# One ring of PSUM tiles for all stages, and K in bundles of four: a convolution and channel mix fused on one core

## The chip, the cores, the metric

One core of one Trainium2 chip runs the whole kernel. The metric is device time in microseconds (us); lower is better. Each time below is the median of the runs named beside it. TensorE does the matmuls, VectorE (DVE) and ScalarE (ACT) read their results out of PSUM, GpSimd (POOL) and SyncE (SP) mostly issue transfers.

## The reference, cut to what matters

```python
# x: (8, 4160, 192) f32; 8 heads of 24 channels, 7 taps each
w = softmax(weight, axis=-1)
y[b, s, h, :] = sum(w[h, k] * x_pad[b, s + k, h, :] for k in range(7))   # causal
xk = mu_k * y + (1 - mu_k) * y_prev       # y_prev: y one token earlier
xr = mu_r * y + (1 - mu_r) * y_prev
k = relu(xk @ w_k)                        # 192 -> 1024
v = (k * k) @ w_v                         # 1024 -> 192
out = sigmoid(xr @ w_r) * v
```

## The kernel before

The eight sequences go through in four pairs. A pair is cut into steps of 512 tokens (the first pair begins and ends with a step of 256) and a tail of 64 tokens, because 4160 is 8 x 512 + 64. For each step TensorE computes, interleaved with its neighbours in time:

- the convolution `ps_c` (a matmul with a banded matrix), which ScalarE copies to `y`; `y` goes to DRAM and comes back transposed as `yT` (the first groups of the first pair are transposed on TensorE instead);
- K (`ps_k`) in slots of 2 x 512 columns, whose relu is on ScalarE and whose square is on VectorE;
- R (`ps_r`) with its sigmoid on ScalarE;
- V (`ps_v`) from the squares; VectorE multiplies it by the sigmoid into `o_sb`, which is stored.

From `yT` VectorE makes the difference `d` and the mixes `xk` and `xr`. The contraction of K is 192 = 128 + 64: a "hi" matmul of full height, and a "lo" pair of half height that runs side by side on the two halves of the array (row-tiled; in the trace they have 64 rows each, and the two of a pair start 3 or 4 ns apart, where two of full height and 512 columns start 216 apart). Parts that the change touches, cuts marked with `# ...`:

```python
psK = ctx.enter_context(tc.tile_pool(name="psK", bufs=3, space=bass.MemoryType.PSUM))  # K, R, conv: 3 x 2 banks
psV = ctx.enter_context(tc.tile_pool(name="psV", bufs=2, space=bass.MemoryType.PSUM))  # V, transposes: 2 x 1 bank

def k_section(ns):                 # a bundle: three slots (or two)
    # ...
    for n in ns[:-1]:
        k_mm(n, True, True)        # hi
    for n in ns[:-1]:
        k_mm(n, False, False)      # lo, row-tiled
    k_mm(ns[-1], False, True)      # lo, row-tiled
    k_mm(ns[-1], True, False)      # hi

def r_mm(m0):                      # R of four tiles, or of a tail, in a tile of psK
    ps = psK.tile([P, 2, BANK], FP32, tag="k", name="ps_r")
    # ...
def v_mm(m):                       # V of one tile of 128 tokens; a pair shares a bank of psV
    # ...
    if t % 2 == 0:
        v_ps[q] = psV.tile([P, 2, D], FP32, tag="v", name="ps_v")
    # ...

# the schedule, by slots n
at(dve, xs[-1] + 1, y_write, g)
at(dve, xs[-1] + (3 if g == 4 else 9), y_read, g)   # the transposed read, 8 slots after the write
# ...
at(xt, 2 if s == 0 else vs - 3, r, m)               # R and its sigmoid, 3 slots ahead of V
at(pe, vs, v_mm, m)                                 # V, one tile at a time
```

Of the kernel before, what the change touches and what calls it, by code (L numbers as in the profile page):

```python
# [14 lines left out]
def kernel(  # L15
# [29 lines left out]
    WARM = 20  # L45
# [5 lines left out]
    eight = ctx.enter_context(tc.tile_pool(name="eight", bufs=8))  # L51
    psK = ctx.enter_context(tc.tile_pool(name="psK", bufs=3, space=bass.MemoryType.PSUM))
    psV = ctx.enter_context(tc.tile_pool(name="psV", bufs=2, space=bass.MemoryType.PSUM))
# [17 lines left out]

    groups = []
    for p in range(NPAIR):
        blk0 = 0
        for nb, s, on_pe in (
            ((3, 0, True), (4, 1, True), (4, 2, True), (5, 3, True), (10, 4, False), (9, 6, False))
            if p == 0
            else ((10, 0, False), (10, 2, False), (10, 4, False), (5, 7, False))
        ):
            groups.append((p, blk0, nb, steps[first_step[p] + s][3], on_pe))  # L80
            blk0 += nb
# [52 lines left out]
    w_all = const.tile([P, H, K, 8], FP32)  # L134
# [61 lines left out]
    def make_toe():  # L196
# [4 lines left out]
            in0=w_nrm.unsqueeze(3).to_broadcast([P, H, K, 8]),  # L201
            in1=bass.AP(tensor=m.tensor, offset=m.offset, ap=[m.ap[0], [0, H], [1, K], [1, 8]]),
            op=ALU.mult,
        )
        with nc.allow_low_precision(reason="a sum of one number and zeros"):
            nc.vector.tensor_reduce(
                out=w_per,
                in_=w_all.rearrange("p h k r -> p h r k"),
                axis=mybir.AxisListType.X,
                op=ALU.add,  # L210
            )
# [18 lines left out]
    def conv_mm(g, c):  # L230
        nb = groups[g][2]
        if c == 0:
            ys[g] = two.tile([P, GB, 2 * D], BF16, tag="y", name="y")
        ps2 = psK.tile([P, 2, BANK], FP32, tag="k", name="ps_c")
        for k, hs in enumerate(chunks(g)[c : c + 2]):
# [3 lines left out]
            for i, h in enumerate(hs):  # L239
# [6 lines left out]
                )  # L246

# [40 lines left out]
    tr_ps = {}  # L288

    def tr_mm(g, j):  # L290
# [3 lines left out]
        ps = psV.tile([P, 3, 2, BLK], BF16, tag="v", name="ps_t")  # L294
        tr_ps[g, j] = ps
        for i in range(min(2, nb - 2 * j)):
            for c in range(3):
                nc.tensor.transpose(
                    out=ps[:, c, i, :],
                    in_=ys[g][:BLK, 2 * j + i, c * P : (c + 1) * P],  # L300
                    identity=ident[:BLK, :BLK],
                )

    def tr_out(g, j, copy):
        p, blk0, nb, _, _ = groups[g]
        ps = tr_ps.pop((g, j))
        n = min(2, nb - 2 * j)
        c0 = YC + (blk0 + 2 * j) * BLK
        copy(  # L309
            out=yTs[p][:, :, c0 : c0 + n * BLK].rearrange("p c (n t) -> p c n t", n=n),  # L310
            in_=ps[:, :, :n, :],
        )
# [16 lines left out]
    def mix(s, i, part):  # L329
# [4 lines left out]
        if part == 0 and L > TAIL:  # L334
            if i == 0:
                xks[s] = two.tile([P, 3, STEP], BF16, tag="xk", name="xk")
            else:
                xrs[s] = three.tile([P, 3, STEP], BF16, tag="xr", name="xr")
# [29 lines left out]
    def k_mm(n, hi, start):  # L368
# [5 lines left out]
        if start:  # L374
            k_ps[n] = psK.tile([P, 2, BANK], FP32, tag="k", name="ps_k")
# [15 lines left out]
    def k_section(ns):  # L391
# [4 lines left out]
        for n in ns[:-1]:  # L396
            k_mm(n, True, True)
        for n in ns[:-1]:
            k_mm(n, False, False)
        k_mm(ns[-1], False, True)  # L400
        k_mm(ns[-1], True, False)

    def k_mm_tail(n, p):
        ps = psK.tile([P, NF, 2 * TAIL], FP32, tag="k", name="ps_k")
# [38 lines left out]
    tiles = []  # L443
    for s, (p, t0, L, n0, ns) in enumerate(steps):
        for t in range(max(1, 2 * L // P)):
            at_ = n0 + ns + 1
            tiles.append((s, t, max(at_, tiles[-1][2] + 1) if tiles else at_))

    r_ps, r_sbs, v_ps = {}, {}, {}


    def r_mm(m0):
        s, _, _ = tiles[m0]
        p, _, L, _, _ = steps[s]
        ps = psK.tile([P, 2, BANK], FP32, tag="k", name="ps_r")
        r_ps[m0] = ps
        for k in range(4 if L > TAIL else 1):
            t = tiles[m0 + k][1]
            o = ps[:, k // 2, k % 2 * D : (k % 2 + 1) * D]
            if L > TAIL:  # L460
                xr = xrs[s]
                st, c = divmod(t * P, L)
                hi, lo, wlo = xr[:, st, c : c + P], xr[:, 2, c : c + P], wr[:, 2 + st, :]
            else:
                hi, lo, wlo = tails[p % 2][:, 1, 1, :], tails[p % 2][:, 1, 0, :], wr[:, 1, :]
            nc.tensor.matmul(out=o, lhsT=hi, rhs=wr[:, 0, :], start=True, stop=False)  # L466
            nc.tensor.matmul(out=o, lhsT=lo, rhs=wlo, start=False, stop=True)  # L467

    def r_sig(m0):
        ps = r_ps.pop(m0)  # L470
        if steps[tiles[m0][0]][2] > TAIL:
            r_sb = three.tile([P, 2, 2 * D], BF16, tag="r_sb", name="r_sb")
            nc.scalar.activation(out=r_sb, in_=ps[:, :, 0 : 2 * D], func=AF.Sigmoid)  # L473
            for k in range(2):
                r_sbs[m0 + 2 * k] = r_sb[:, k, :].rearrange("p (t d) -> p t d", t=2)
        else:
            r_sb = two.tile([P, D], BF16, tag="r_tail", name="r_tail")
            nc.scalar.activation(out=r_sb, in_=ps[:, 0, 0:D], func=AF.Sigmoid)
            r_sbs[m0] = r_sb.unsqueeze(1)

    def v_mm(m):
        s, t, _ = tiles[m]
        q = m - t % 2
        if t % 2 == 0:
            v_ps[q] = psV.tile([P, 2, D], FP32, tag="v", name="ps_v")
        o = v_ps[q][:, t % 2, :]
        k2 = k2s[s]
        for f in range(NF):
            nc.tensor.matmul(  # L489
                out=o,  # L490
                lhsT=k2[:, f, t * P : (t + 1) * P],
# [5 lines left out]
    def v_out(m):  # L497
        s, t, _ = tiles[m]
        p, t0, L, _, _ = steps[s]
        n = 2 if L > TAIL else 1  # L500
        o_sb = eight.tile([P, 2, D], FP32, tag="o_sb", name="o_sb")
        nc.vector.tensor_tensor(  # L502
            out=o_sb[:, :n, :], in0=v_ps.pop(m)[:, :n, :], in1=r_sbs.pop(m)[:, :n, :], op=ALU.mult
        )
        if L > TAIL:
            st, c = divmod(t * P, L)
            nc.sync.dma_start(
                out=out[2 * p + st, t0 + c : t0 + c + 2 * P, :].rearrange("(m p) d -> p m d", p=P),
                in_=o_sb,
            )  # L510
        else:
            for i in range(2):
                nc.sync.dma_start(
                    out=out[2 * p + i, t0:S, :], in_=o_sb[i * TAIL : (i + 1) * TAIL, 0, :]
                )


    early, xt, pe, dve = ({} for _ in range(4))

    def at(table, n, fn, *a):  # L520
        table.setdefault(n, []).append((fn, a))
# [6 lines left out]
    def r(m0):  # L528
        r_mm(m0)
        r_sig(m0)  # L530

    def tr(g, j):
        tr_mm(g, j)
        tr_out(g, j, nc.vector.tensor_copy)

    for g, (p, blk0, nb, n0, on_pe) in enumerate(groups):
        nx = -(-len(chunks(g)) // 2)
        ntr = (nb + 1) // 2
        if g == 0:
            continue  # L540
        if g == 1:
            xs, trs = [], [0] * ntr
        elif on_pe:
            xs = [[0, 1], [4, 6]][g - 2]
            trs = [[2, 3], [7, 8, 9]][g - 2]
        else:
            xs = {28: [7, 9, 11, 13], 44: [14, 16, 18, 20]}[n0] if p == 0 else range(n0 - 38, n0 - 38 + 4 * nx, 4)
            trs = []
            at(dve, xs[-1] + 1, y_write, g)

            at(dve, xs[-1] + (3 if g == 4 else 9), y_read, g)
        if g > 3:

            n = {4: 4, 5: 5, 6: 9, 7: 32, 8: 42, 9: 53}.get(g) or steps[first_step[p]][3] + (-63, -47, -31, -14)[(g - 6) % 4]
            at(early, n, x_tile, g, nc.vector)
            at(early, n, load_x, g)
        for i, n in enumerate(xs):
            at(xt, n, conv, g, 2 * i)
        for j, n in enumerate(trs):
            at(pe, n, tr, g, j)  # L560
    for s, (p, t0, L, n0, ns) in enumerate(steps):
        if s == 0:
            when = (None, None, None, 1, 1)
        elif s == 1:
            when = (0, 0, 1, 4, 5)
        elif s == 2:
            when = (5, 6, 7, 9, 10)
        elif n0 == 28:
            when = (22, 24, 25, 27, 28)
        else:  # L570
            when = (n0 - 8, n0 - 6, n0 - 5, n0 - 3, n0 - 2)
        if when[0] is not None:
            at(dve, when[0], diff, s)
        for n, (i, part) in zip(when[1:], ((0, 0), (0, 1), (1, 0), (1, 1))):
            if n is not None:
                at(dve, n, mix, s, i, part)
    for m, (s, t, vs) in enumerate(tiles):
        if t % 4 == 0:
            at(xt, 2 if s == 0 else vs - 3, r, m)
        if t % 2 == 1 or steps[s][2] == TAIL:  # L580
            at(dve, vs + 1, v_out, m - t % 2)
        at(pe, vs, v_mm, m)

    def run(table, n):
        for fn, a in table.get(n, ()):
            fn(*a)

    def warm(n):
        ps = psV.tile([P, BANK], FP32, tag="v", name="warm")
        for _ in range(n):  # L590
            nc.tensor.matmul(out=ps, lhsT=ones_t, rhs=zeros, start=True, stop=True)  # L591

    def prologue():
# [38 lines left out]
        dve_, act_ = nc.vector.tensor_copy, nc.scalar.copy  # L632
# [85 lines left out]
```

## Time and profile before

| | before |
|---|---|
| time, first three runs | 454.83 us (454.81 to 454.86) |
| span in the trace | 453.3 us |
| busy: TensorE, VectorE, ScalarE | 97%, 85%, 78% |
| granted TensorE clock | 1.00 |

Timeline columns: start, duration, engine, line, operation, output<-inputs, shapes, count, and in brackets the idle time before it and what ended it.

### The profile page before, as it was taken

The numbers are of one execution on the slowest core, as the hardware profiler recorded it, in microseconds if no ns is written. First come the engines' busy times: TensorE is split into PE (matmuls) and PEld (weight loads), VectorE is DVE, ScalarE is ACT, GpSimd is POOL, SyncE is SP. The second block draws the span as 40 slices with busy tenths as digits, with TensorE's granted clock in tenths as the row PEclk, the third lists the DMA queues.
The fourth block names the chain that finished last, engine by engine and source line by source line (L and its number), as shares of the span: only waits on it lengthen the run. The fifth ranks groups of instructions, "written<-read, shape, count | busy, mean of one in ns | idle before, by whom it ended". The sixth has DMA issues, their size and how long they took to land.

```text
span 453.3 us, 10019 instructions
## 1 busy us (share of the span) xinstructions
PE 441.0 (97%) x3942; PEld 301.8 (67%) x3942; DVE 385.1 (85%) x762; ACT 355.8 (78%) x464; POOL 48.6 (11%) x70
## 2 busy tenths in 40 slices
PE   7889999999999999999999999999999999999996
PEld 3555666767876676676676776776676776767676
DVE  4799489897989879888998888897998997988963
ACT  3779987888887787888887887888887877767771
POOL 8550001102030100102020010100200000000000
PEclk9999999999999999999999999999999999999999
DMA  8999869799598694957769793957655573421223
GB/s 90 146 170 137 149 190 168 151 192 186 135 179 177 165 180 108 156 137 145 170 140 161 182 184 108 147 135 189 111 135 136 142 152 94 109 71 53 72 71 97
DMA packets 134177, 63.66 MB, mean 140 GB/s; under 512 B 85714, under 2 KB 133874, under 8 KB 134130
## 3 DMA queue, kind: packets, MB, share of 16 engines
q1 hardware_dynamic: 95906, 48.33, 43.0%
q0 software_dynamic: 38224, 14.68, 28.5%
q8 instruction: 31, 0.51, 0.5%
q14 instruction: 16, 0.13, 0.1%
HBM read 29.39 MB, written 36.99 MB: 146 GB/s over the span
## 4 chain that ended last, share of the span: by engine, by line
PE 87%; DVE 8%; DMA 3%; ACT 1%; issue 1%; DVEq 0%
PE ps_k L383 36%; PE ps_v L489 35%; PE ps_r L466 4%; PE ps_r L467 4%; PE ps_c L240 4%; DVE k L440 3%; PE warm L591 2%; DMA yT<-y_dram 2%; DMA y_dram<-y 1%; DVE d L322 1%; DVE yT L309 1%; PE ps_k L409 1%; DVE o_sb L502 1%; DVE xk L364 1%; DVE xr L361 1%
## 5 line engine op out<-in xcount | busy, mean ns | idle before, releaser
L421 ACT ACTIVATE k_sb<-ps_k 128x1024 bf16<-128x1024 f32 x260 | 248.3, 1025 | 56.6 <-PE ps_k L383 52.6
L383 PE MATMUL ps_k<-xk,wk 128*128 128x512 bf16 (+3 forms) x1056 | 199.3, 374 | 0.5 <-ACT k_sb L421 0.4
L489 PE MATMUL ps_v<-wv,k 128*128 128x192 bf16 x2048 | 195.1, 246 | 2.3 <-DVE k L440 1.0
L489 PEld LDWEIGHTS <-k 128*128 128x128 bf16 x2048 | 172.8, 98 | 26.6 <-DVE k L440 1.6
L440 DVE TENSOR_TENSOR k<-k_sb 128x1024 bf16<-128x1024 bf16 x256 | 172.3, 684 | 4.6 <-ACT k_sb L421 4.3
L383 PEld LDWEIGHTS <-wk 128*128 128x128 bf16 (+1 forms) x1056 | 63.0, 96 | 104.7 <-issue 72.8
L502 DVE TENSOR_TENSOR o_sb<-ps_v,r_sb 128x384 f32<-128x384 f32 x128 | 70.9, 554 | 43.2 <-PE ps_v L489 41.0
L473 ACT ACTIVATE r_sb<-ps_r 128x768 bf16<-128x768 f32 x64 | 52.8, 825 | 16.9 <-PE ps_r L467 14.9
L466 PE MATMUL ps_r<-wr,xr 128*128 128x192 bf16 x256 | 47.5, 246 | 1.1 <-DVE xr L364 1.0
L260 ACT CAST y<-ps_c 120x480 bf16<-120x480 f32 (+5 forms) x85 | 39.7, 527 | 11.1 <-PE ps_c L240 11.1
L112 POOL DMA_DIRECT2D xb<-in_x_dram x36 | 32.4, 905 | 147.7 <-PE ps_k L383 61.8
L467 PE MATMUL ps_r<-wr,xr 128*128 128x192 bf16 x256 | 47.4, 246 | 0.3 <-DVE xr L364 0.3
L364 DVE TENSOR_TENSOR xr<-xr,yT 128x1024 bf16<-128x1024 bf16 (+1 forms) x66 | 36.3, 549 | 2.3
L364 DVE TENSOR_TENSOR xk<-xk,yT 128x1024 bf16<-128x1024 bf16 (+1 forms) x66 | 36.2, 549 | 2.3
L322 DVE TENSOR_TENSOR d<-yT 128x1536 bf16<-128x1536 bf16 (+2 forms) x37 | 31.6, 853 | 3.6 <-DMA yT<-y_dram 3.5
L240 PE MATMUL ps_c<-xb,toe 128*128 128x480 bf16 (+4 forms) x144 | 31.8, 322 | 0.9 <-DMA xb<-in_x_dram 0.8
L361 DVE TENSOR_SCALAR xk<-d,mu 128x1024 bf16<-128x1024 bf16 (+1 forms) x66 | 27.6, 418 | 0.2
L361 DVE TENSOR_SCALAR xr<-d,mu 128x1024 bf16<-128x1024 bf16 (+1 forms) x66 | 27.1, 411 | 0.0
L467 PEld LDWEIGHTS <-xr 128*128 128x128 bf16 x256 | 25.0, 98 | 2.4 <-issue 1.7
L466 PEld LDWEIGHTS <-xr 128*128 128x128 bf16 x256 | 25.0, 98 | 1.8 <-DVE xr L364 1.2
L263 ACT CAST y<-ps_c 120x480 bf16<-120x480 f32 (+7 forms) x47 | 21.5, 509 | 0.8 <-DVE yT L268 0.6
L240 PEld LDWEIGHTS <-toe 128*128 128x128 bf16 x144 | 12.7, 98 | 2.2 <-issue 1.5
(55 smaller groups left out, 81.8 us busy)
## 6 DMA issues: line engine op xcount, KB each, us to landing
out_dram<-o_sb SPq DMA_DIRECT2D x128, 192.0 KB, 2.5
y_dram<-y SPq DMA_DIRECT2D x10, 900.0 KB, 7.0
xb<-in_x_dram POOLq DMA_DIRECT2D x14, 480.0 KB, 8.7
xb<-in_x_dram POOLq DMA_DIRECT2D x6, 432.0 KB, 8.8
xb<-in_x_dram POOLq DMA_DIRECT2D x10, 192.0 KB, 4.5
y_dram<-y SPq DMA_DIRECT2D x3, 450.0 KB, 4.0
y_dram<-y SPq DMA_DIRECT2D x1, 810.0 KB, 7.1
xb<-in_x_dram POOLq DMA_DIRECT2D x2, 384.0 KB, 7.1
```

Of the source, the lines that this page charges most:

```text
L240: nc.tensor.matmul(out=ps[:, :, :, i * G : (i + 1) * G], lhsT=toe[:, h, :], rhs=xbs[g][:, :nb, :, h * G : (h + 1) * G], start=True, stop=True,
L260: copy(out=yh[:, :, :, c0 : c0 + n], in_=ps[:BLK, :, :, 0:n])
L361: nc.vector.tensor_scalar(out=o, in0=d[:, sl, :L], scalar1=mu[:, i, part : part + 1], scalar2=None, op0=ALU.mult)
L364: nc.vector.tensor_tensor(out=o, in0=o, in1=yT[:, sl, c0 : c0 + L], op=ALU.add)
L383: nc.tensor.matmul(out=ps[:, i, f * L : (f + 1) * L], lhsT=wk[r, 0 if hi else 1, fs], rhs=xk[r, i if hi else 2, :L], start=start and f == ...
L421: nc.scalar.activation(out=k_sb, in_=ps.rearrange("p a b -> p (a b)"), func=AF.Relu)
L440: nc.vector.tensor_tensor(out=o, in0=i, in1=i, op=ALU.mult)
L466: nc.tensor.matmul(out=o, lhsT=hi, rhs=wr[:, 0, :], start=True, stop=False)
L467: nc.tensor.matmul(out=o, lhsT=lo, rhs=wlo, start=False, stop=True)
L473: nc.scalar.activation(out=r_sb, in_=ps[:, :, 0 : 2 * D], func=AF.Sigmoid)
L489: nc.tensor.matmul(out=o, lhsT=k2[:, f, t * P : (t + 1) * P], rhs=wv[:, f, :], start=(f == 0), stop=(f == NF - 1),)
L502: nc.vector.tensor_tensor(out=o_sb[:, :n, :], in0=v_ps.pop(m)[:, :n, :], in1=r_sbs.pop(m)[:, :n, :], op=ALU.mult)
```

## The change

The intent: step into the row-tiled stretch once per four slots in place of once per three; make V's products twice as wide; and let every stage share the eight banks of PSUM that both kernels use (3 x 2 + 2 x 1 before, 4 x 2 now), so that none stands idle while another is short. The whole schedule is thereby counted in bundles of four slots and no longer in slots. The diff, cut to its core:

```diff
-    psK = ctx.enter_context(tc.tile_pool(name="psK", bufs=3, space=bass.MemoryType.PSUM))
-    psV = ctx.enter_context(tc.tile_pool(name="psV", bufs=2, space=bass.MemoryType.PSUM))
+    ring = ctx.enter_context(tc.tile_pool(name="ring", bufs=4, space=bass.MemoryType.PSUM))
 ...
-        for n in ns[:-1]:
+        for n in ns[:2]:
             k_mm(n, True, True)
-        for n in ns[:-1]:
+        for n in ns[:2]:
             k_mm(n, False, False)
-        k_mm(ns[-1], False, True)
-        k_mm(ns[-1], True, False)
+        for n in ns[2:]:
+            k_mm(n, False, True)
+        for n in ns[2:]:
+            k_mm(n, True, False)
 ...
+            quads.append((s, j, last_bundle[s] + 1 + j + (s == 0 or L == TAIL and p < NPAIR - 1)))
 ...
+    def four_tiles(mm, s, j, name):
+        ps = ring.tile([P, 2, BANK], FP32, tag="k", name=name)
+        for k in range(4):
+            mm(ps[:, k // 2, k % 2 * D : (k % 2 + 1) * D], s, 4 * j + k)
+        return ps[:, :, 0 : 2 * D]
 ...
+    def v_tail(s):
+        p, t0, L, _, _ = steps[s]
+        ps = ring.tile([P, 2, BANK], FP32, tag="k", name="ps_vt")
+        r_mm(ps[:, 1, 0:D], s, 0)
+        r_sb = two.tile([P, D], BF16, tag="r_tail", name="r_tail")
+        nc.scalar.activation(out=r_sb, in_=ps[:, 1, 0:D], func=AF.Sigmoid)
+        v_mm(ps[:, 0, 0:D], s, 0)
+        o_sb = two.tile([P, D], FP32, tag="o_tail", name="o_tail")
+        nc.vector.tensor_tensor(out=o_sb, in0=ps[:, 0, 0:D], in1=r_sb, op=ALU.mult)
 ...
-            at(dve, xs[-1] + 1, y_write, g)
-            at(dve, xs[-1] + (3 if g == 4 else 9), y_read, g)
+            xs = range(fb - 9, fb - 9 + nx)
+            at(late, xs[-1], y_write, g)
+            at(late, xs[-1] + (1 if g == 4 else 2), y_read, g)
```

Cut away: the mixes a bundle ahead, the prologue (a reduction without a stride, 16 matmuls named `warm` for 20, on zeros and with a result that nothing reads, copies split over two engines), fewer buffers for `xr` and `o_sb`, and the last store on a second queue. In one bundle the order is: K of four slots with its relus, V, mixes, three squares, V's product, then convolution with its copies and R with its sigmoid, the last square, and the writes and reads of `y`.

## The prediction

> **What bounds the kernel now.** I read the page's busy line first, then the stretches of the span, then the chain of waits, then the start of the timeline, because the first only says who is busy and the last says who makes whom wait.
>
> ```profile
> PE 441.0 (97%) x3942; PEld 301.8 (67%) x3942; DVE 385.1 (85%) x762; ACT 355.8 (78%) x464; POOL 48.6 (11%) x70
> ...
> 0.00:40.00 40.00, 33.29 (x243) 18.33 (x244) 31.48 (x72) 26.87 (x45) 22.59 (x38) 1.00 1.23 146
> 40.00:80.00 40.00, 38.68 (x342) 26.45 (x341) 32.18 (x62) 33.31 (x46) 1.88 (x2) 1.00 0.81 156
> 80.00:120.00 40.00, 40.00 (x360) 27.65 (x358) 34.56 (x74) 33.85 (x46) 4.50 (x6) 1.00 0.93 168
> 240.00:280.00 40.00, 40.00 (x360) 27.61 (x359) 34.61 (x67) 31.82 (x40) 2.00 (x2) 1.00 0.81 163
> ```
>
> TensorE is without a gap from about 70 us to the end, at full clock (the 1.00); VectorE and ScalarE have about 14% and 18% to spare there. Only the first 70 us have idle TensorE. But "busy" is not "streaming at its peak", so I count what the matmuls must take. The chain of waits gives start-to-start times of whole stretches:
>
> ```profile
> 199.88 2.15 PE ps_k L383 x12
> ...
> 224.81 1.51 PE ps_k L383 x8
> 226.32 1.32 PE ps_v L489 x16
> ```
>
> A V matmul takes 1.32/16 = 82.5 ns[...]. A bundle of three K slots has six full-height matmuls and three pairs of half-height ones that run side by side: 9 x 215.8 = 1.94 us, and it took 2.15. A bundle of two: 6 x 215.8 = 1.29, and it took 1.51. So about **0.2 us per bundle, whatever its length**, is not streaming. It is the step into the row-tiled stretch and out of it.
>
> The whole sum of streaming, counts from the lines by form: V 2,080 and R 520 at 82.5 ns = 214.5; K of 512 columns, 496 full and 248 pairs, at 215.8 = 160.6; K of 256 columns 48 at 109.2 = 5.2; K tails 64 at 55.8 = 3.6; convolution 22.8; 48 transposes 2.5: **409 us**. The first convolution starts at 8.45 us and the last matmul ends at 449.04: 440.6 us. So 31.5 us are not streaming: 88 bundles x 0.2 = 17.6, and **13.9 us of stalls**[...]. Nearly all of these stalls are in the first 70 us, and the timeline says who is waited for:
>
> ```profile
> 20.16 0.26 PE L466 MATMUL ps_r<-wr,xr 128*128 128x192 bf16 x1 [0.99 <-DVE xr L364]
> 24.72 0.57 PE L240 MATMUL ps_c<-xb,toe 128*128 128x240 bf16 x4 [0.81 <-DMA xb<-in_x_dram]
> 30.65 0.82 PE L489 MATMUL ps_v<-wv,k 128*128 128x192 bf16 x8 [0.86 <-DVE yT L309]
> 68.90 0.92 PE L489 MATMUL ps_v<-wv,k 128*128 128x192 bf16 x9 [0.98 <-DVE k L440]
> ```
>
> VectorE is what TensorE waits for while the pipeline fills.
>
> [...] the product o_sb took 554 ns for 384 columns and 0.36 us for 192, so 1.04 ns a column and some 0.15 us fixed.
>
> **The change part by part.**
> *Bundles of four.* 256 slots in 64 bundles in place of 88. The streaming is the same; 24 x 0.2 = **-4.8 us**, all on TensorE, which sets the end. A bundle takes 4 x 0.647 + 0.2 = 2.8 us.
> *V in quads.* The same matmuls. VectorE makes 64 products of 768 columns (0.554 + 384 x 1.04 ns = 0.95 us, estimate) for 128 of 0.554: 70.9 - 61 = 10 us less VectorE work. Off the path where TensorE has no gaps: 0 there.
> *The ring.* A bundle now asks for tiles in the order k k k k v, convolution, r, and each waits for the reader of the tile four earlier. I walked a steady bundle with convolution. From its start T: K to 2.8, V to 5.43, convolution to 5.84, R to 6.5. ScalarE's four relus run at 0.91 us apiece from T+1.39 (as at 64.36 to 65.75 before) to 5.15, the two copies from 6.03 to 7.05, the sigmoid to 7.85; the tile it frees is wanted by the next bundle's fourth slot at T+8.1. VectorE, heavy bundle: difference and xk 2.86, three squares to 5.4, the product right after V to 6.4, which the next second slot wants at 6.93; the last square to 7.0. Two bundles of VectorE: 1.0 + 2 x 1.86 + 8 x 0.62 + 2 x 0.9 = 11.5 us of TensorE's 12.2 without and 13.0 with convolution. It fits, with 0.25 to 0.5 us to spare: **0**.
> *Pair boundaries.* The second bundle of a pair has no V: TensorE K 2.8 + convolution 0.41 + tail 0.83 + R 0.66 = 4.7 us. ScalarE has 4 x 0.91 + 1.02 + 0.33 + 0.8 = 5.8. The ring gives no room to run ahead, so TensorE waits about 1.0 us for copies and relus; before lost 0.15 there. Three boundaries: **+2.5 us**.
> *Prologue.* The reduction that makes the Toeplitz weights read with a stride and took 0.95 us; 448 columns in a row should take 0.62 (128x56 took 0.21). With 16 warm matmuls in place of 20 the first convolution then waits for its x, landed at 8.15 (from the landing times of the issues): 8.2 for 8.45. Copies split over two engines and separate tiles let the first difference start sooner; but the K weights land at 13.2 (upper rows) and 14.3 (lower), so K starts at 13.4 for 14.11: **-0.7 us**.
> *Start, K to step 4.* I walked bundles 0 to 7. VectorE stays what is waited for: xk of step 1 is there at 20.2, the first product frees its ring tile only at 37.5 after a difference, a mix and three squares (TensorE stands 2 us), and the transposed y of group 4 comes back at about 60 for 57.7. Stalls of 8.8 us from the first K to 65 us for 9.4 before: **-0.6**, good to no more than 2.5.
> *End.* The last tail's two stores go out on two queues; before the second was issued 0.56 us after the first: **-0.4**.
> Sum: -4.8 - 0.7 - 0.6 + 2.5 - 0.4 = -4.0.
>
> **The rivals.**
> *The single ring stalls each bundle.* In its favour: one order for all stages, slack of 0.25 us, and before's own waits at 37.8 us are of this kind. If 0.15 us were lost in each of 64 bundles, 10 us come back: 460. Against: the walk fits, ScalarE is 80% busy and VectorE loses 10 us of work.
> *The start gains more than I see.* The schedule there is set by hand for each group, so it was tuned; with VectorE 10 us lighter and mixes a bundle ahead the 13.9 us of stalls could fall to 8: 444.
> *VectorE becomes the bound.* 11.5 of 12.2 us without convolution, which is the last 40 us or so; a few hundred ns a bundle would give 452 to 454.
>
> **Range and chances.** 454.8 - 4.0 is 450.8. My walks take each hand-off at its longest, so I lean by 0.8: **450.0 us**. Low 445.5: no loss at the boundaries and 2 us more at the start. High 453.5: the ring costs most of what the switches give. Faster by over 2% means below 445.7: 0.13. Slower by over 2%, above 463.9, needs over 0.2 us lost in every bundle: 0.03. Within 2%: 0.84.
>
> **What would show it.** K stretches of 16 matmuls in 2.8 us; the convolution at 8.2; K at 13.4; products of 0.95 us; TensorE gaps of about 1 us at each boundary, put down to ScalarE; TensorE without gaps otherwise after 66 us. Wrong if K stretches take over 3 us, if V or K waits for VectorE or ScalarE in most bundles, or if the start has stalls of under 6 or over 12 us.

The matmuls named `warm`: their time is counted in the 13.9 us of stalls. The sum: -4.8 - 0.7 - 0.6 + 2.5 - 0.4 = -4.0, and with the lean of 0.8 that is 450.0. The traces themselves have what the count of streaming rests on: in the kernel before, from the start of a matmul to the start of the next that follows at once, 215.8 ns on average for 512 columns, 109.2 for 256, 82.5 for 192 and 55.8 for 128. They also have the 0.2 us of a bundle: from the last 512-wide start of full height to the first of half height it is 312 ns (median), and from the last of half height to the next of full height 308, in place of 216 each, so 0.19 us for both.

## More of the kernel before

TensorE sets the end, so what counts is which other engine it ever waits for. The view of waits for TensorE of the kernel before (columns: who waited, for whom; us in total, how often, the longest) has nothing over 1.6 us, and what there is lies in the filling of the pipeline:

```profile
PE warm L591 <- DVE zeros L601: 1.6, 1, 1.6
PE ps_r L466 <- DVE xr L364: 1.0, 1, 1.0
PE ps_v L489 <- DVE k L440: 1.0, 1, 1.0
```

For what follows, one place in the kernel before deserves a look: the tail at the end of the first pair.

```profile
135.64 0.25 PE L466 MATMUL ps_r<-wr,tail 128*128 128x192 bf16 x1
135.72 0.25 PE L467 MATMUL ps_r<-wr,tail 128*128 128x192 bf16 x1
136.00 0.33 ACT L478 ACTIVATE r_tail<-ps_r 128x192 bf16<-128x192 f32 x1 [0.25 <-PE ps_r L467]
140.50 0.82 PE L489 MATMUL ps_v<-wv,k2t 128*128 128x192 bf16 x8
```

R of the tail is in a tile of one pool and V in a tile of the other. V comes 4.2 us after the sigmoid has ended, with no bracket behind it: it waited for nothing.

## The result, and the profile after

| | before | after |
|---|---|---|
| time, median of 4 | 454.82 us (454.44 to 454.86) | 467.85 us (466.12 to 473.19) |
| ratio, fast runs | 1 | 1.0276 [1.0238, 1.0314] |
| span in the trace | 453.3 us | 464.4 us |

Ratios here and below are the mean time of one kernel's fast runs over the mean of the other's fast runs of the same rounds, with a 95% interval, so they are not quite the ratio of the medians quoted. The changed kernel is slower by 2.8%. Its run of 473.19 us is slow (granted clock 0.978); the other three are fast, at 0.994, 0.989 and 0.991. The profiled run is the one of 466.12 us.

The page's busy line of the changed kernel has 3.6 us less of TensorE busy and 3.2 us more of VectorE than before:

```profile
PE 437.4 (94%) x3940; PEld 305.1 (66%) x3940; DVE 388.3 (84%) x699; ACT 354.1 (76%) x465; POOL 48.1 (10%) x70
```

The stretches of the span say where it stands still (columns: from:to, length, busy us of PE, PEld, DVE, ACT and POOL with the number of instructions, granted clock, DMA share, GB/s):

```profile
114.00:146.00 32.00, 27.05 (x263) 19.80 (x260) 25.22 (x48) 22.08 (x33) 3.42 (x5) 1.00 0.95 168
...
245.00:262.00 17.00, 14.27 (x108) 8.77 (x106) 12.26 (x22) 11.49 (x17) 3.11 (x4) 0.90 0.88 147
260.00:340.00 80.00, 80.00 (x726) 56.32 (x724) 72.14 (x127) 65.55 (x86) 6.38 (x8) 1.00 0.71 144
340.00:370.00 30.00, 26.08 (x238) 17.91 (x237) 22.81 (x42) 22.61 (x31) 0.00 (x0) 1.00 0.56 129
```

(VectorE's products fell from 70.9 to 61.2 us by their durations, as foreseen, and the engine is still not less busy. Durations of successive instructions there lie over one another in the records, and in a sum they are counted twice: by the records of both traces the sum of all durations fell from 428.4 to 419.6 us, and the part counted twice from 43.3 to 31.3. From its start to the next start, where that followed at once, a narrow product took 0.468 us (median) and a wide one 0.875. So two narrow ones cost 0.06 more than one wide one, some 4 us in all, an estimate from 64 x 0.06, and not 10.)

In the middle of a pair, 260 to 340, TensorE has no gap: the ring costs nothing there. Around each change of pairs, at about 140, 250 and 360, it loses 2.7 to 5.0 us. A steady bundle in the chain of waits (start, duration, what) is as planned, K in 2.80, V in 2.64:

```profile
97.36 2.80 PE ps_k L406 x16
100.16 2.64 PE ps_v L488 x32
102.80 0.41 PE ps_c L250 x2
```

I summed the intervals between the starts of successive matmuls in both traces and took off the streaming time of each form (from start to start where the next follows at once, in both traces: 215.8 ns on average for 512 columns, 109.1 to 109.2 for 256, 82.5 for 192, 55.8 for 128; the prediction counted with the same). The streaming is 410.0 us in both; the first matmul starts at 1.6 us in both. The rest:

| us | before | after | change |
|---|---|---|---|
| steps into and out of the row-tiled stretch | 16.5 | 12.0 | -4.5 |
| gaps up to 80 us, warm matmuls counted in | 18.7 | 16.3 | -2.4 |
| gaps after 80 us | 2.1 | 20.4 | +18.3 |
| after the start of the last matmul | 4.45 | 4.15 | -0.3 |
| sum | | | +11.1 |

The span grew by 464.4 - 453.3 = 11.1. So the gain that was planned is there, and 18.3 us of new gaps swallow it. The view of waits of the changed kernel, TensorE's and VectorE's, names the gaps' main owners:

```profile
PE ps_vt L488 <- ACT r_tail L534: 8.6, 4, 2.7
PE ps_v L488 <- DVE o_sb L515: 2.8, 2, 1.6
...
PE ps_k L406 <- DVE o_sb L515: 2.1, 1, 2.1
...
DVE d L345 <- DMA yT<-y_dram: 6.7, 4, 2.8
```

**The tail.** The timeline of the changed kernel at the first tail, to be held against the four lines of before:

```profile
137.91 3.85 ACT L446 ACTIVATE k_sb<-ps_k 128x1024 bf16<-128x1024 f32 x4
...
140.06 0.24 PE L484 MATMUL ps_vt<-wr,tail 128*128 128x192 bf16 x1
...
141.54 0.87 ACT L286 CAST y<-ps_c 120x480 bf16<-120x480 f32 x2
142.16 0.58 ACT L289 CAST y<-ps_c 120x320 bf16<-120x320 f32 x1
142.47 0.50 ACT L534 ACTIVATE r_tail<-ps_vt 128x192 bf16<-128x192 f32 x1
143.02 0.82 PE L488 MATMUL ps_vt<-wv,k2t 128*128 128x192 bf16 x8 [2.72 <-ACT r_tail L534]
```

R's last matmul is at 140.06. The sigmoid has to queue behind four relus and three copies on ScalarE and starts at 142.47. V does not need the sigmoid, and it writes bank 0 while the sigmoid reads bank 1, and yet it starts at 143.02, when the sigmoid is over. The trace's record of V's first matmul says the same: it carries a wait on the semaphore that ScalarE's instructions, the sigmoid among them, update.

From start to start less the streaming this is 2.88 us at each of the three pair changes and 0.58 at the last tail, 9.2 us.

**The late read.** The same timeline an earlier stretch on. The transposed read of a group, issued by SyncE, and what waits for it:

```profile
76.03 3.93 SPq L309 DMA_TRANSPOSE yT<-y_dram  x1
...
85.46 0.96 DVE L345 TENSOR_TENSOR d<-yT 128x1536 bf16<-128x1536 bf16 x1 [2.80 <-DMA yT<-y_dram]
...
88.31 1.89 DVE L465 TENSOR_TENSOR k<-k_sb 128x1024 bf16<-128x1024 bf16 x3
90.12 0.95 DVE L515 TENSOR_TENSOR o_sb<-ps_v,r_sb 128x768 f32<-128x768 f32 x1
91.13 2.53 PE L406 MATMUL ps_k<-xk,wk 128*128 128x512 bf16 x14 [2.06 <-DVE o_sb L515]
```

VectorE is ready for `d` at 82.66 and gets `yT` at 85.46, over 9 us after the issue. Mixes, squares and the product follow 2.8 us late. Only the product frees the tile of V, the ring has no other, and K's second slot stands for 2.06. In the kernel before a read has up to 20 us to spare: one was issued at 98.70, had landed at 107.04 and was used at 127.27. The 14 reads there take 4.1 to 9.2 us from issue to landing (median 6.6); in the changed kernel they take 4.4 to 10.0 (median 8.7), so they also became slower, and why is not tested. The product was late in this way at 88.7, 235 and 346.7 us: 2.2 + 1.7 + 1.35 = 5.3 us.

**The clock.** After one of the tail waits TensorE ran at half its clock, as two stretches of the changed kernel show (clock is the third value from the right):

```profile
250.00:253.70 3.70, 0.98 (x12) 0.83 (x11) 2.62 (x6) 2.88 (x6) 1.72 (x3) 1.00 1.27 258
253.70:257.20 3.50, 3.50 (x17) 1.71 (x16) 2.83 (x6) 0.81 (x1) 0.00 (x0) 0.51 1.61 191
```

The low stretch is 3.41 us long, and in it 512-wide matmuls start 427 ns apart and 192-wide ones 160, for 216 and 82 elsewhere, so about 1.7 us of work is lost. (The slow run's lower clock, 0.978 against 0.994, is 0.016 of 471 us, 7.5 us, and it took 7.1 longer; no trace of it is kept.)

The other two waits of 2.72 us, at 143 and 364, were not followed by such a stretch, and the traces show a difference. In all twelve kept traces a stretch at full clock that ends within the kernel lasts a multiple of 3.413 us (here 249.17 = 73 x 3.413 and 204.80 = 60 x 3.413), so in these traces the clock changes on a fixed grid. I cut the traces into windows of this grid, from the first full clock to the last matmul, and summed the time in which TensorE has no matmul in each. Eight windows have 2.04 to 2.72 us of it, and a half-clock stretch follows every one; all others have 1.93 or less, and none is followed by one. The wait before 252.93 lies in one window, with 2.61 us; the two others are split by a boundary of the grid, and no window there has more than 1.93 and 1.59.

What is left of the 20.4: 1.5 before K of the first tail, 1.4 in the first pair change (0.49 + 0.65 + 0.24), and 1.2 spread. 9.2 + 5.3 + 1.8 + 1.5 + 1.4 + 1.2 = 20.4.

### The profile page after: what moved, and what is told of

Its sections match the earlier page's. It is cut to its first block, busy times and chain, and to the rows that moved or that the text cites. A ratio compares the mean times of both kernels' runs of the same rounds, so it can differ in the third digit from the quotient of the medians.

```text
span 464.4 us, 9771 instructions
## 1 busy us (share of the span) xinstructions
PE 437.4 (94%) x3940; PEld 305.1 (66%) x3940; DVE 388.3 (84%) x699; ACT 354.1 (76%) x465; POOL 48.1 (10%) x70
## 4 chain that ended last, share of the span: by engine, by line
PE 64%; DMA 8%; DVE 5%; ACT 3%; issue 2%; SPq 0%; DVEq 0%; ACTq 0%
PE ps_v L488 28%; PE ps_k L406 27%; DMA yT<-y_dram 6%; PE ps_r L484 3%; PE ps_r L483 3%; DMA xb<-in_x_dram 2%; PE ps_c L250 2%; ACT k_sb L446 2%; DVE k L465 2%; DVE o_sb L515 1%; PE ps_vt L488 1%; DVE d L345 1%; DVE xk L384 1%; DVE xk L387 0%; PE ps_k L434 0%
## 5 line engine op out<-in xcount | busy, mean ns | idle before, releaser
L446 ACT ACTIVATE k_sb<-ps_k 128x1024 bf16<-128x1024 f32 x260 | 245.7, 1033 | 19.0 <-PE ps_k L406 12.3
L406 PE MATMUL ps_k<-xk,wk 64*128 64x512 bf16 (+3 forms) x1056 | 192.3, 375 | 5.7 <-DVE xk L387 2.1
L488 PE MATMUL ps_v<-wv,k 128*128 128x192 bf16 x2048 | 179.4, 246 | 3.4 <-DVE o_sb L515 2.8
L488 PEld LDWEIGHTS <-k 128*128 128x128 bf16 x2048 | 170.7, 98 | 17.2 <-issue 3.7
L465 DVE TENSOR_TENSOR k<-k_sb 128x1024 bf16<-128x1024 bf16 x256 | 168.6, 686 | 12.3 <-ACT k_sb L446 11.1
L406 PEld LDWEIGHTS <-wk 64*128 64x128 bf16 (+1 forms) x1056 | 66.7, 96 | 107.1 <-issue 60.8
L515 DVE TENSOR_TENSOR o_sb<-ps_v,r_sb 128x768 f32<-128x768 f32 x64 | 61.2, 957 | 31.6 <-PE ps_v L488 31.6
L286 ACT CAST y<-ps_c 120x480 bf16<-120x480 f32 (+6 forms) x84 | 38.6, 521 | 41.4 <-PE ps_c L250 41.4
L289 ACT CAST y<-ps_c 120x480 bf16<-120x480 f32 (+6 forms) x45 | 20.7, 508 | 8.9 <-PE ps_c L250 8.9
```

Of the source, the lines that this page charges most:

```text
L286: copy(out=yh[:, :, :, c0 : c0 + n], in_=ps[:BLK, :, :, 0:n])
L406: nc.tensor.matmul(out=ps[:, i, f * L : (f + 1) * L], lhsT=wk[r, 0 if hi else 1, fs], rhs=xk[r, i if hi else 2, :L], start=start and f == ...
L446: nc.scalar.activation(out=k_sb, in_=ps.rearrange("p a b -> p (a b)"), func=AF.Relu)
L465: nc.vector.tensor_tensor(out=o, in0=i, in1=i, op=ALU.mult)
L488: nc.tensor.matmul(out=o, lhsT=k2s[s][:, f, t * P : (t + 1) * P], rhs=wv[:, f, :], start=(f == 0), stop=(f == NF - 1),)
L515: nc.vector.tensor_tensor(out=o_sb.rearrange("p (b t) d -> p b (t d)", b=2), in0=v_ps.pop((s, j)), in1=r_sbs.pop((s, j)), op=ALU.mult,)
```

## The experiments

**Theory.** Two waits that the new schedule brought in make the loss: V of a tail behind the sigmoid of its own ring tile, and transposed reads issued one bundle before their use. **Rivals.** The ring as such is too short (four tiles for all stages); or ScalarE's excess work at a pair change, which the prediction had put at 2.5 us, is larger than thought, and the waits only stand where it would show anyway; or the bundle of four brought less than it should. All experiments are edits of the changed kernel, and all gave correct results. The trace of each is that of one run; where the text speaks of the clock of other runs it goes by their mean clock alone. "Before" ran beside them at medians of 454.29 to 454.78.

### A ring tile of its own for the tail's R

```diff
-        ps = ring.tile([P, 2, BANK], FP32, tag="k", name="ps_vt")
-        r_mm(ps[:, 1, 0:D], s, 0)
+        ps_r = ring.tile([P, 2, BANK], FP32, tag="k", name="ps_rt")
+        r_mm(ps_r[:, 0, 0:D], s, 0)
         r_sb = two.tile([P, D], BF16, tag="r_tail", name="r_tail")
-        nc.scalar.activation(out=r_sb, in_=ps[:, 1, 0:D], func=AF.Sigmoid)
+        nc.scalar.activation(out=r_sb, in_=ps_r[:, 0, 0:D], func=AF.Sigmoid)
+        ps = ring.tile([P, 2, BANK], FP32, tag="k", name="ps_vt")
         v_mm(ps[:, 0, 0:D], s, 0)
```

> The changed kernel, with R of a tail in a ring tile of its own in place of the second bank of V's tile. Theory (V of a tail waits for the sigmoid because both lie in one tile): the four waits of 2.88, 2.88, 2.88 and 0.58 us go, and with them the stretch at half clock (about 1.8 us in the profiled run); some of ScalarE's excess at a pair boundary comes back, up to 1 us each. From 466.1 us of the profiled run to 454 to 457 us, granted clock 1.000 in every run, and runs that agree within 0.3%. Rival (the clock falls for another reason, or the single ring is what waits): the time stays over 462 us and the clock stays under 1.

Measured: 460.17 us (459.19 to 462.66), ratio 1.0136 [1.0104, 1.0169]. The direction is right and the size missed. The timeline of this kernel at the same tail:

```profile
139.47 0.24 PE L484 MATMUL ps_rt<-wr,tail 128*128 128x192 bf16 x1
140.31 0.82 PE L488 MATMUL ps_vt<-wv,k2t 128*128 128x192 bf16 x8 [0.59 <-ACT k_sb L446]
```

V no longer waits for the sigmoid, but for a relu to free the ring tile that it now needs, 0.59 in place of 2.72; and further gaps of 0.26 and 0.32 come up right behind it, the second put down to one of ScalarE's copies. Each of the three pair changes gave 1.33 us back (0.75 from start to start, 0.26, 0.32), 4.0 in all. The profiled runs agree: 466.12 - 9.2 (tail waits) - 1.7 (the half clock, gone in this run) + 4.0 = 459.2, measured 459.19. That it fits so closely is partly luck: the late products came to 4.5 us here and not 5.3, and other small changes made up for it. So the wait was worth what it showed, but part of it had hidden ScalarE's excess. This also says that the order alone was not the cause: R, sigmoid and V still stand in that order, and in two tiles V does not wait for the sigmoid.

### The transposed read one bundle earlier

```diff
-            at(late, xs[-1] + (1 if g == 4 else 2), y_read, g)
+            at(late, xs[-1] + 1, y_read, g)
```

> The changed kernel, with the transposed read of y issued one bundle earlier for all groups. Theory (the read lands after the difference that needs it, VectorE then hands its product and squares over late): VectorE's four waits for yT, 6.7 us, and TensorE's four gaps behind them (2.2, 1.5, 1.7 and 1.4 us, 6.8 in all) go; tail waits and half clock stay: 458 to 461 us. Rival (these gaps are ScalarE's or the ring's): no change within 2 us.

Measured: 463.97 us (462.69 to 464.23), ratio 1.0202 [1.0180, 1.0224]. No difference waits for `yT` any more and the three late products are gone, 5.3 us. The gap of 1.5 before the tail's K stays as 1.26: it was not the read's doing. The total missed what was expected, because now a half-clock stretch follows every one of the three tail waits and not one; all four runs have a clock of 0.989. The first of them, in two stretches of this kernel:

```profile
138.00:142.00 4.00, 1.25 (x14) 1.10 (x14) 2.70 (x6) 3.02 (x6) 1.80 (x3) 1.00 1.27 166
142.00:145.50 3.50, 3.28 (x16) 1.53 (x16) 2.74 (x6) 1.12 (x2) 0.00 (x0) 0.51 1.46 187
```

-5.3 + 2 x 1.7 = -1.9, and the profiled run went from 466.12 to 464.23.

### Both

The two edits together.

> Both of the two edits before in one kernel. Theory (the two waits add up and are all that was missed): 449 to 452 us, the 450 that was predicted, granted clock 1.000. Rival (something in the ring takes their place): over 455 us.

Measured: 455.14 us (454.30 to 456.17), ratio 1.0018 [0.9997, 1.0039], clock 0.996 to 1.0. Against the changed kernel's three fast runs (median 466.90) the two edits bring 11.8 us, nearly all of the loss. By the ratios that is 0.0258, more than the sum of each alone, 0.0140 and 0.0074, since the half-clock stretches go with the waits. But the time expected was 449 to 452. The waits of this kernel name what remains at the pair changes:

```profile
PE ps_vt L488 <- ACT k_sb L446: 1.8, 3, 0.6
...
PE ps_k L434 <- DVE o_sb L515: 1.1, 1, 1.1
```

From start to start, the first pair change loses 1.26 + 0.49 + 0.65 + 0.24 + 1.33 = 4.0 and the two others 1.33 each: 6.6 us, where the prediction had +2.5. Of these the 1.26 is a wait for VectorE's product (the second line above); most of the rest is put down to ScalarE. Both theory and rival hold a part: the two waits with the clock that falls behind them are 11.8 us net, and the excess at the pair changes, larger than thought, takes back what the bundles of four saved.

### Two visits to the row-tiled stretch per bundle

This doubles the cost that the bundle of four was to save, on top of both edits.

```diff
         for n in ns[2:]:
-            k_mm(n, False, True)
+            k_mm(n, True, True)
         for n in ns[2:]:
-            k_mm(n, True, False)
+            k_mm(n, False, False)
```

> Both edits, and each bundle of four goes into the row-tiled mode twice, two slots each, in place of once. Theory (a visit costs a fixed 0.19 us that nothing hides): 64 x 0.19 = 12 us more than the kernel with both edits, 461 to 464 us; K stretches of 2.99 us for 2.80. Rival (the visit is hidden by other waits, so that the bundle size saved nothing): within 3 us of it.

Measured: 467.01 us (466.21 to 467.49), ratio 1.0277 [1.0258, 1.0295], 11.9 over the version with both edits. One K stretch and the V after it, first in this kernel, then in the version with both edits:

```profile
285.38 3.07 PE L406 MATMUL ps_k<-xk,wk 128*128 128x512 bf16 x15
288.38 2.81 PE L488 MATMUL ps_v<-wv,k 128*128 128x192 bf16 x32
```

```profile
279.11 2.97 PE L406 MATMUL ps_k<-xk,wk 128*128 128x512 bf16 x15
281.92 2.31 PE L488 MATMUL ps_v<-wv,k 128*128 128x192 bf16 x26
```

From K's start to V's start: 288.38 - 285.38 = 3.00, against 281.92 - 279.11 = 2.81 (the traces lack a few records here, as the counts show, but the first matmul of each stretch is there). 0.19 x 64 bundles = 12.2, measured 11.9. The third rival falls: a visit costs 0.19 us and every one of it reaches the end, so 24 visits fewer did save the 4.5 us.

### V of the first pair's last step one bundle later

The first pair change is dearer than the others because its last step has 256 tokens: the tail and V follow closer. On top of both edits:

```diff
-            quads.append((s, j, last_bundle[s] + 1 + j + (s == 0 or L == TAIL and p < NPAIR - 1)))
+            quads.append((s, j, last_bundle[s] + 1 + j + (L < STEP and p < NPAIR - 1)))
```

> The kernel with both edits, and the V quad of pair 0's last half step one bundle later, so that the bundle of the tail has one quad and not two and the next bundle has one and not none. Theory (what is left at a pair boundary is ScalarE, whose relus, copies and sigmoids take longer than TensorE's work in a bundle that has no V): the first boundary's gaps of 1.26, 0.49, 0.65 and 0.24 us shrink to under 1 us in sum; 1.5 to 2.5 us less than the kernel with both edits, 452.6 to 453.6 us. Rival (the gaps come from the transfers or from VectorE's mixes): within 0.5 us of it.

Measured: 453.56 us (452.79 to 454.22), ratio 0.9977 [0.9957, 0.9996]. That is 1.6 less than with both edits, within what was expected. The waits of 0.49 and 0.65 at the first pair change are gone, and so are the 1.26 and 0.24; one of 1.02, V's wait for VectorE's product, comes up at 124 us. The clocks are 0.994 to 0.998.

### And one convolution unit out of the crowded bundle

On top of that, one of the convolution units with its copies goes into the tail's short bundle, so that ScalarE has fewer copies in the bundle after it.

```diff
+            if (g - 6) % 4 == 2:
+                xs = [fb - 9, fb - 9, fb - 8, fb - 6]
```

> As the run with the V quad later, and the convolution unit whose copies fall in the second bundle of each pair moved to the tail's bundle, where ScalarE has some 1.8 us to spare. Theory (ScalarE): each of the three boundaries wins about 1 us of its gaps (0.75, 0.26 and 0.32 us in the second and third): 2 to 3 us less than that run, 450 to 451 us, below the kernel before by 0.8 to 1%. Rival: no change, or the tail's bundle gets longer by the same amount.

Measured: 453.21 us (451.50 to 454.26), ratio 0.9971 [0.9945, 0.9998]. It missed. At each pair change the gap of 0.75 fell to 0.41 and that of 0.32 to 0.26, so 0.40 each time and 1.2 us in all, where 2 to 3 were expected. A half-clock stretch at 21 us in the profiled run, and by the clocks (0.996, 0.999, 0.995, 0.992) in most, blurs the total. ScalarE's copies are therefore not all of the boundary's cost.

### V of the tail ahead of the sigmoid, in the same tile

This tells the tile from the ring. The read is issued a bundle earlier, R and V of a tail share their ring tile as in the changed kernel, but V is issued first.

```diff
+        v_mm(ps[:, 0, 0:D], s, 0)
         r_mm(ps[:, 1, 0:D], s, 0)
         r_sb = two.tile([P, D], BF16, tag="r_tail", name="r_tail")
         nc.scalar.activation(out=r_sb, in_=ps[:, 1, 0:D], func=AF.Sigmoid)
-        v_mm(ps[:, 0, 0:D], s, 0)
```

> The changed kernel with the read one bundle earlier, tail still in one ring tile, but its V matmuls issued ahead of its R matmuls and of the sigmoid. Theory (the wait is on the tile: whatever writes it after a reader was issued waits for that reader, though the reader is in the other bank): no wait for the sigmoid is left, the clock stays at full speed at the boundaries, and the time is that of the kernel with both edits within 1.5 us: 453.5 to 456 us. Rival (V of the tail waits for its ring slot or for the squares): the time stays at that of the kernel with the earlier read alone, 464 us.

Measured: 454.16 us (453.91 to 454.43), ratio 0.9994 [0.9977, 1.0011]. The timeline of this kernel at the same tail:

```profile
139.02 0.82 PE L488 MATMUL ps_vt<-wv,k2t 128*128 128x192 bf16 x8
...
139.75 0.25 PE L484 MATMUL ps_vt<-wr,tail 128*128 128x192 bf16 x1
```

No bracket: nothing is waited for, with the same tile, the same two banks and the same data. What made V wait, 2.72 us in the changed kernel, was a write issued after a read of the same tile, not the data and not the bank: in the first experiment another tile took the wait for the sigmoid away, here another order does.

### All of these

V ahead of the sigmoid, the read earlier, V of the half step later and the convolution unit moved. This differs from the sixth experiment only in the tail: V ahead of R in one ring tile here, R ahead of V in two there.

> Earlier read, V of the tail ahead of the sigmoid in one tile, V quad of the half step later, convolution copies earlier. Theory: as the run with the copies earlier, or up to 1 us better for the ring tile that it does not use: 449 to 451 us. Rival (the boundary is limited by ring tiles and not by ScalarE): over 1.5 us better than that run.

Measured: 451.64 us (450.87 to 452.14), ratio 0.9939 [0.9922, 0.9956], 1.57 us less than the sixth experiment with its second tile. That is just over the 1.5 set for the rival, and the ranges of the two overlap. The traces are clearer: there each pair change loses 0.41 + 0.26 + 0.26 = 0.93 around the tail, here 0.49. So the second tile, or the order that goes with it, costs about 0.45 us each time; the two were changed together and are not told apart. The copies hold another part of the excess.

### The gap of the first bundle filled

In the timeline of the last kernel, TensorE stands 2.51 us in the first bundle (the line with the bracket at 20.49 below), and a half-clock stretch follows at 21.9; the other runs' clocks (0.999, 0.996, 0.996) suggest it in two of them. Here eight warm matmuls fill that gap.

```diff
             run(xt, b)
+            if b == 0:
+                warm(8)
```

> The best run so far (all four edits), with eight matmuls on zeros put into TensorE's gap of 2.7 us at 17.7 us, where it waits for xk of the second step. They do no work and the wait stays. Theory (the clock falls to one half for 3.4 us because TensorE stood idle for over 2 us shortly before): the stretch at half clock at about 21.9 us goes, granted clock 0.998 or more in all runs, and the time falls by 0.8 to 1.3 us, to 450.3 to 451.0. Rival (the half clock has nothing to do with the gap): no change, or longer by the few matmuls that come late.

Measured: 451.24 us (450.97 to 451.25), ratio 0.9922 [0.9906, 0.9939]. The half-clock stretch is gone and the runs lie within 0.28 us in place of 1.27. By the medians the gain is only 0.4, less than expected; but the two ran in different rounds, and by their ratios to before it is 0.0017, 0.8 us, the low end of what was expected, with intervals that overlap. The filling itself seems to cost a little: K of step 1 starts at 20.67 for 20.49.

### The first bundle's transposes between its slots

The gap itself rather than its consequence: `xk` of the next step waits for transposes that stand behind all four K slots of the first bundle. They go after the second slot. (The warm matmuls of the ninth experiment are not in this kernel.)

```diff
-            if ns:
-                k_section(ns)
-            for n in ns:
-                k_relu(n)
-            run(first, b)
+            if b == 0:
+                k_section(ns[:2])
+                for n in ns[:2]:
+                    k_relu(n)
+                run(first, b)
+                k_section(ns[2:])
+                for n in ns[2:]:
+                    k_relu(n)
+            else:   # as it was
```

> The best run so far (all four edits), with the first bundle's transposes after its second slot in place of its fourth, which gives that bundle two row-tiled stretches. Theory (the gap at 17.7 us is the chain transposes, copies, difference, xk, and it begins when the transposes do): xk of the second step comes 1.2 us earlier, minus 0.2 for the second stretch, and the gap gets short enough that the clock stays up: 449.3 to 450.3 us. Rival (ScalarE's relus and copies hold the second bundle as well): under 0.5 us of gain.

Measured: 450.05 us (449.59 to 450.35), ratio 0.9897 [0.9882, 0.9912]. The K stretch of step 1, first in the kernel with "all of these", then with this edit on top:

```profile
20.49 3.84 PE L406 MATMUL ps_k<-xk,wk 128*128 128x512 bf16 x14 [2.51 <-DVE xk L387]
```

```profile
19.11 2.98 PE L406 MATMUL ps_k<-xk,wk 128*128 128x512 bf16 x15 [1.33 <-DVE xk L387]
```

It starts 1.38 us earlier, and the median fell by 1.6 (the rounds differ; by the ratios, 1.9 us); the half-clock stretch is gone from this trace too. This version beats both kernels: it is 1.0% faster than before and, by the ratios (0.9897 over 1.0276, from different rounds, so roughly), 3.7% faster than the change as given.

## Why the prediction was wrong

It said 450.0 (445.5 to 453.5) and gave slower by over 2% a chance of 0.03; it was 467.85.

- **Bundles of four, -4.8: right.** -4.5 in the two traces; the fourth experiment confirms it from the other side, 0.19 us a visit.
- **V in quads, 0.95 us a product and nothing on the path: right in size** (0.957 on average by the groups). The relief of "10 us less VectorE work" did not show in VectorE's busy time, 388.3 for 385.1: it was worked out from durations that overlap, and from start to start it is some 4 us. VectorE did not become the bound all the same: between 365 us and the last tail TensorE has no gap over 0.2. And the wide product does sit on the path once `d` is late: it frees the only tile that K can have.
- **The ring, 0 in the steady state: right.** Without a gap from 260 to 340 us. The first rival falls for the steady state; when a product is late, and at the pair changes, the ring does count.
- **Prologue, -0.7 and start, -0.6: better than said together**, -2.4 in gaps up to 80 us. The reduction took 0.62 us over columns in a row, for 0.95 with a stride, as foretold. K started at 13.18 (13.4 foretold) and step 1's `xk` was there at 20.1 (20.2). But the stand of 2 us foretold at 37.5 did not come, the largest gap near it being 0.50, so the walk was right only in part.
- **End, -0.4: right**, -0.3.
- **Pair boundaries, +2.5: this is the step that failed.** "TensorE K 2.8 + convolution 0.41 + tail 0.83 + R 0.66" counts the tail as 0.83 us of work with no wait in it. The tail's V waits for the tail's sigmoid, which stands last in ScalarE's queue: 2.88 us at three boundaries and 0.58 at the last tail, 9.2, and a half-clock stretch of 1.7 behind one of them (three in the second experiment). The diff shows it: R, sigmoid and V of one tile in that order. The prediction has no word on that tile. The first and seventh experiments show that the sharing and the order together make the wait. With that wait gone, the excess that the step did foresee came out: 1.33 at each boundary and 2.6 more at the first, 6.6 for 2.5 in the third experiment, 4.1 too much. In the seventh, which keeps the one tile, the second and third boundaries lose 0.26 + 0.55 = 0.81 each, about what the step has for one, and there mechanism and size were right; the first loses 3.7. So what was not in the sum is the first boundary's half step, with 1.26 of it a wait for VectorE and not ScalarE, and in the third experiment that kernel's second ring tile, about 0.5 at each boundary.
- **Transposed reads: left out.** The start's term follows "the transposed y of group 4"; the same question was not asked for the other groups. The change reads them one bundle, some 6.6 us, ahead of their last moment, and a read took over 9 us to land at 76.03: 5.3 us. The kernel before had up to 20 us to spare, which no wait in its profile shows.
- **The sum.** With both waits taken out the time was 455.1 and not 450: 4.1 of these 5 us are the boundaries' term. With the boundary and the first bundle mended, it came to 450.05; that this is the number foretold is chance, since those edits were not in the kernel that was predicted.

What stays open: why fewer of VectorE's durations overlap with half as many products; why the transposed reads take longer in the changed kernel; and how the remaining boundary cost divides between copies, ring tile and order.

## What to carry to other kernels

When a change puts two results into one tile, ask for every write to it which reads of that tile were issued ahead of it and where they stand in the reader's queue: here banks that don't overlap were no answer, and V stood for 2.72 us until a read of the other bank was over. Issue the long producer before the reader of the other half (the seventh experiment: no wait left), or give each its own tile if the ring has one to spare (the first: 0.59 us left, for a ring tile). When a schedule changes its unit of counting, compare for every transfer the distance from issue to use, in microseconds, old against new: here up to 20 us from landing to use before, and after the change a read that landed over 9 us from its issue where the schedule gave it some 6.6. Slack shows in no wait of a profile until it is gone; the time from landing to use shows it.
